# A fused attention and feed-forward kernel: v split one operand per step and passed on through DRAM, seven products in the second layer from a pair's first step on

## The chip, the cores and the metric

The kernel runs on one core of a Trainium2 chip. The metric is the device time of one execution in microseconds (us). The engines are named as in the profile: PE multiplies matrices (PEld loads its weights), DVE and ACT work on vectors, POOL is not used here, and SP issues the transfers (DMA) through one queue.

## The reference

Four batches of 6080 tokens with 256 channels pass through a channel attention and then through a feed-forward network with 2048 hidden units.

```python
# attention: q, k, v are (4, 6080, 256), scores are 256 x 256 per batch
qn = q / (norm(q, axis=1) + 1e-06)
kn = k / (norm(k, axis=1) + 1e-06)
a = softmax(kn.T @ qn / tau)
x = v @ a
# feed-forward, w_in 256 x 2048, w_out 2048 x 256
h = x @ w_in
out = 0.5 * h * (1 + erf(h / sqrt(2))) @ w_out
```

All is float32.

## The kernel before

**Numbers.** Each float32 operand of a product is split into a high part (a cast on ACT) and a low part (a difference on DVE), and a product is three passes on PE: high by high, high by low, low by high. The attention is folded into the first layer: for each batch, softmax(scores) times w_in gives that batch's first weights, so that the first layer is v times these.

**Tiles.** A pair is two blocks of n = 512 tokens (480 in a batch's last pair); each batch has six, written (b,p). A pair runs through eight steps u; in a step two tiles of 128 hidden units are made. So there are 192 steps, (b,p,u). Within a step PE's code alternates between the first layer of step u and the second layer of the step before: `slot` 0 to 6 count the seven products of the first layer (`first_products`, `do(0)` to `do(6)`, by the table `ORDER`), and after each of them one or two groups of `second_products` are put in, each of three matmuls. Behind every step come the stages `EDGE` and `EDGE + 1`.

**Seven products.** The first layer is one level of Strassen's scheme in Winograd's form: seven products of half blocks in place of eight, 21 matmuls of n columns. It needs seven operands from v: the blocks B11, B21, B22 and the sums T1 to T4 (`v_sum`), each split (`v_split`) into tiles vh and vl. In pair (0,0) `plain_products` makes the first layer with eight products from B11, B21, B12, B22. The second layer has four groups for the token block j = 1 (12 matmuls of n columns), then for j = 0 either four more plain groups (12 matmuls of n columns) or the same scheme with seven products (21 matmuls of n/2 columns, on `ws`, sums of w_out, and on sums of the hidden values that `sums` makes on DVE and ACT). `strassen(b,p,u)` says which: seven products for all u but 0, from pair (0,2) on.

**Accumulators.** The plain groups add into the PSUM tiles c10, c11 (j = 1) and c00, c01 (j = 0), the seven products into p0, p1 and also into c00 and c01. Behind a pair's last step `evict` copies c10 and c11 out (in step u=0 of the next pair), and in its step u=1 `combine` forms the results of p0 and p1 in osb (one copy on ACT, four operations on DVE) and `merge` adds c00 and c01 to it. Only then may the next pair write these tiles.

**v.** `load_v` brings 1 MB of a pair's v into v_raw; the four sums are made in steps u=3 to 6 of the pair before, and the seven splits in its step u=7 and the next pair's step u=0, each shortly after the product that last used the old tile.

**Other work beside it.** While a batch runs, the scores of the next are gathered: `load_qk`, `split_qk` (tiles hl) and `burst` (16 matmuls between two steps), `norm_part` (norms of the columns), `softmax`, and the next batch's first weights (`w_part`, `w_split`). In batch 3 there is none of this. The weights w_out of a step (wo, 512 KB, and ws, 512 KB) are read back from DRAM for every step by `ahead`, wo two steps and ws one step before use; there are two buffers of each.

**Order.** `at(step, slot, job)` puts a job behind a slot, `run` calls it there, and `spread` puts the stages of a generator behind later slots (12 is slot 2 of the next step). From pair (0,1) on the orders of PE, DVE and ACT are those in which the code issues; the order of SP's queue is found by a scheduler from a model of its own.

Of the kernel before, what the change touches and what calls it, by code (L numbers as in the profile page):

```python
# [9 lines left out]
F32 = mybir.dt.float32  # L10
F32R = mybir.dt.float32r
# [3 lines left out]
ALU = mybir.AluOpType  # L15
AX = mybir.AxisListType

P = 128
B, N, C = 4, 6080, 256
DFF = 2048  # L20
NT = 512
NJ = -(-N // P)
NFT = DFF // P
NCT = C // P
# [41 lines left out]
def channel_attention_gelu_ffn(ctx, tc, qk, kqt, vt, tau, w_in, w_out, out):  # L66
# [29 lines left out]
    def f32(ap):  # L96
        return ap.bitcast(F32)
# [405 lines left out]

    def load_v(b, p):
        t0, n = PAIRS[p]
        raw = pv.tile([P, NCT, 2 * NT], F32, name="v_raw")
        nc.sync.dma_start(out=raw[:, :, :2 * n],
                          in_=vt[:, b * N + t0:b * N + t0 + 2 * n].rearrange("(t p) n -> p t n", p=P))
        vraw[b, p] = raw

    def v_blocks(b, p):
        n = PAIRS[p][1]
        raw = vraw[b, p]
        return {(k, j): raw[:, k, j * n:(j + 1) * n] for k in range(2) for j in range(2)}

    def v_sum(b, p, i):
        n = PAIRS[p][1]
        x = v_blocks(b, p)
        if i == 0:
            vts[b, p] = [pv.tile([P, NT], F32, name=f"vs{k}") for k in range(4)]  # L520
        ts = [t[:, :n] for t in vts[b, p]]
        to, x0, x1 = ((0, x[0, 1], x[0, 0]), (2, x[1, 1], x[0, 1]), (1, x[1, 1], ts[0]), (3, x[1, 0], ts[1]))[i]
        dve.tensor_tensor(out=ts[to], in0=x0, in1=x1, op=ALU.subtract)

    def v_split(b, p, i):
        n = PAIRS[p][1]
        x = v_blocks(b, p)
        src = {B11: x[0, 0], B21: x[1, 0], B22: x[1, 1]}.get(i)
        if (b, p) == (0, 0) and i == B12:
            src = x[0, 1]  # L530
        if src is None:
            src = vts[b, p][i - T1][:, :n]
        hi = pv.tile([P, NT], F32R, name=f"vh{i}")
        lo = pv.tile([P, NT], F32R, name=f"vl{i}")
        vops[b, p, i] = hi, lo
        act.copy(out=hi[:, :n], in_=src)
        yield
        dve.tensor_tensor(out=lo[:, :n], in0=src, in1=f32(hi[:, :n]), op=ALU.subtract)

# [11 lines left out]
        passes(ps[:, :n], whs[g][:, a, q], wls[g][:, a, q], hi[:, :n], lo[:, :n], start, stop)  # L553

    def strassen(b, p, u):
        return u > 0 and (b, p) > (0, 1) and (b, p, u) != (B - 1, NP - 1, NU - 1)

    pending = []

# [103 lines left out]
    def plain_products(b, p, u):  # L663

        n = PAIRS[p][1]
        g, q = divmod(u, 2)
        out = state["blocks"] = {}
        wh, wl = whs[g], wls[g]
        a21 = a21s[g]
        rows = {1: ((wh[:, A11, q], wl[:, A11, q]), (wh[:, A12, q], wl[:, A12, q])),  # L670
                0: ((a21[:, 0, q], a21[:, 1, q]), (wh[:, A22, q], wl[:, A22, q]))}
        cols = {0: (B11, B21), 1: (B12, B22)}
        for j in (1, 0):
            for i in (1, 0):
                ps = bank()
                for k in range(2):
                    hi, lo = vops[b, p, cols[j][k]]
                    passes(ps[:, :n], *rows[i][k], hi[:, :n], lo[:, :n], k == 0, k == 1)
                    if k == 0:
                        yield  # L680
                out[i, j] = gelu(ps[:, :n], n, i, j)
                flush()
                if (i, j) != (0, 0):
                    yield
# [93 lines left out]
    def merge(b, p, c):  # L778

        n = PAIRS[p][1]  # L780
        po = pos[b, p]
        last = (b, p) == (B - 1, NP - 1)
        parts = ((0, n // 2), (n // 2, n)) if last and c == NCT - 1 else ((0, n),)
        for lo, hi in parts:
            y = po["y"][:, c, lo:hi]
            dve.tensor_tensor(out=y, in0=po[f"c0{c}"][:, lo:hi], in1=y, op=ALU.add)
            if last:
                t = b * N + PAIRS[p][0]
                nc.sync.dma_start(out=out[c * P:(c + 1) * P, t + lo:t + hi], in_=y)
        if c == NCT - 1 and not last:  # L790
            store(b, p, 0, po["y"])
# [62 lines left out]
    for js in range(NQS):  # L854
# [5 lines left out]
            load_unit()  # L860
        if js in NARROWS:
            narrow_unit()
    for i in (B11, B21, B12, B22):
        deque(v_split(0, 0, i), 0)
    for x in held:
        keep(*x)
    fill = qk_fill()
# [53 lines left out]
    def at(step, slot, job):  # L921
        jobs.setdefault((step, slot), []).append(job)
# [5 lines left out]
    def spread(gen, step, *slots):  # L928
        for x in slots:
            at(step + x // 10, x % 10, lambda: next(gen, None))  # L930
# [20 lines left out]
        at(s + 1, EDGE, drop)  # L951
    for b in range(1, B):
        base = (b - 1) * NP * NU
        for i in range(2 * NCT * NSC):

            def norm(b=b, i=i, step=base + 8 + i):
                gen = norm_part(b, *divmod(i, NSC))
                with behind("kept"):
                    next(gen)
                at(step + 1, 2, lambda: next(gen, None))  # L960
            at(base + 8 + i, EDGE, norm)

        def soft(step=base + 36):
            gen = softmax(False)
            next(gen)
            spread(gen, step, 12, 10 + EDGE, 22, 26, 20 + EDGE)
        at(base + 36, EDGE, soft)
        for g in range(NWG):
            at(base + 39 + 2 * g, EDGE if g == 0 else EDGE + 1, lambda b=b, g=g: load_win(b, g))
            for m in range(NCT):  # L970
                at(base + 41 + 2 * g + m, EDGE, lambda b=b, g=g, m=m: w_part(b, g, m))

            def wsums(b=b, g=g, step=base + 42 + 2 * g):
                spread(w_split(b, g), step, 10, 11, 12, 20, 22, 23)
            at(base + 42 + 2 * g, EDGE, wsums)
    for b in range(B):
        for p in range(NP):
            nxt = (b, p + 1) if p + 1 < NP else (b + 1, 0)
            base = (b * NP + p) * NU
            if nxt[0] < B:  # L980
                at(base + 1, EDGE, lambda nxt=nxt: load_v(*nxt))
                for i in range(4):
                    at(base + 3 + i, 6, lambda nxt=nxt, i=i: v_sum(*nxt, i))
                for i, (hi, lo) in enumerate(((1, 2), (2, 3), (3, 4), (5, 6), (6, 10), (10, 11), (11, 12))):

                    def vs(nxt=nxt, i=i, step=base + NU - 1, lo=lo):
                        gen = v_split(*nxt, ORDER[i][1])
                        next(gen)
                        spread(gen, step, lo)
                    at(base + NU - 1 + hi // 10, hi % 10, vs)  # L990
                if (b, p) > (0, 1):

                    def end(b=b, p=p, step=base + NU + 1):
                        gen = combine(b, p)
                        next(gen)
                        spread(gen, step, 1)
                        for c in range(NCT):
                            at(step, 2, lambda c=c: merge(b, p, c))
                    at(base + NU + 1, 0, end)

    steps = [(b, p, u) for b in range(B) for p in range(NP) for u in range(NU)]
    second, count, rest = iter(()), 0, iter(())
# [70 lines left out]
```

## Time and profile before

| | us |
|---|---|
| runs shown | 2173.92, 2174.5, 2175.94 (median 2174.5) |
| the profiled execution | 2174.69 |
| its span | 2172.9 |
| PE busy | 2152.8 |
| DVE busy | 1734.9 |
| ACT busy | 1622.5 |

The time of an execution lies 1.8 us over its profile's span. Busy shares are means over very different stages: the first 61 us are loads, norms and the first batch's scores; pair (0,0) follows until 154 us, pair (0,1) until 244 us, and the other 22 pairs run in the same pattern until the end. A plain step takes about 10.4 us, or 11.8 with a burst of scores behind it. A row of the timeline has start, duration, engine, line, operation, the tiles written and read, and their shapes; what stands in brackets is the idle time before it and what ended it. Since one helper records every operation, all rows of the engines have the line L138, and one goes by the tiles; rows of SP have the lines of their own.

### The profile page before, as it was taken

Reading aid. Unit: us, or ns where it says so; the run is one execution under the profiler, and the core shown is the slowest. Engines: PE = TensorE matmul, PEld = TensorE weight load, DVE = VectorE, ACT = ScalarE, POOL = GpSimd, SP = SyncE. Lnnn points to the kernel's source line nnn. Section 1 sums busy time; section 2 is a strip of 40 time slices with the busy share of each in tenths; the row PEclk is TensorE's granted clock in tenths of the full one; section 3 lists DMA queues with packets and bytes.
Section 4 is the critical chain, followed back from the end, with each engine's and each line's share of the span. In section 5 each row is a group of like instructions: output and inputs, shape, how many; then the busy total and the mean of one; then the engine's idle time right before and its main releaser. Section 6 shows DMA issues by size and latency. Waiting matters only on the chain.

```text
span 2172.9 us, 29906 instructions
## 1 busy us (share of the span) xinstructions
PE 2152.8 (99%) x11061; PEld 1822.7 (84%) x11061; DVE 1734.9 (80%) x2732; ACT 1622.5 (75%) x2692; POOL 1.3 (0%) x8
## 2 busy tenths in 40 slices
PE   9999999999999999999999999999999999999999
PEld 8777888887888888888888888888888888888888
DVE  6997788877788788887788878888778777777776
ACT  5767778867777787786777778887677777677675
POOL 0000000000000000000000000000000000000000
PEclk9999999999999999999999999999999999999999
DMA  9545655544344555553434545554344333333332
GB/s 381 180 150 199 213 184 199 183 161 146 136 144 145 176 204 180 199 202 128 140 135 141 173 168 202 184 205 163 106 146 144 118 129 114 127 128 115 125 119 95
DMA packets 100547, 352.18 MB, mean 162 GB/s; under 512 B 10288, under 2 KB 12464, under 8 KB 98352
## 3 DMA queue, kind: packets, MB, share of 16 engines
q1 hardware_dynamic: 100400, 350.27, 46.3%
q8 instruction: 87, 1.43, 0.3%
q14 instruction: 60, 0.49, 0.1%
HBM read 312.74 MB, written 37.49 MB: 161 GB/s over the span
## 4 chain that ended last, share of the span: by engine, by line
PE 87%; DVE 7%; ACT 4%; issue 1%; DMA 0%; DVEq 0%; ACTq 0%; POOL 0%; POOLq 0%
PE h L138 45%; PE c L138 33%; PE p L138 9%; DVE h L138 2%; DVE vl L138 2%; DVE x L138 1%; ACT gh L138 1%; DVE gl L138 1%; ACT x L138 1%; ACT vh L138 1%; ACT g L138 0%; DVE small L138 0%; ACT L138 0%; ACT p L138 0%; DVE osb L138 0%
## 5 line engine op out<-in xcount | busy, mean ns | idle before, releaser
L138 PE MATMUL c<-gh,wo 128*128 128x512 f32 (+3 forms) x2460 | 870.4, 364 | 0.4 <-DVE wo L138 0.4
L138 PE MATMUL h<-vh,wh 128*128 128x512 f32 (+1 forms) x1312 | 520.3, 397 | 12.9 <-DVE h L138 2.8
L138 PEld LDWEIGHTS c<-gh,wo 128*128 128x128 f32 x2460 | 462.2, 188 | 81.9 <-DVE wo L138 1.5
L138 PE MATMUL h<-vh,wl 128*128 128x512 f32 (+1 forms) x1312 | 513.5, 391 | 0.0
L138 PE MATMUL h<-vl,wh 128*128 128x512 f32 (+1 forms) x1312 | 513.5, 391 | 0.0
L138 ACT ACTIVATE gh<-h 128x512 fp32r<-128x512 f32 (+1 forms) x446 | 277.9, 623 | 238.2 <-DVE h L138 219.2
L138 PE MATMUL c<-gl,wo 128*128 128x512 f32 (+3 forms) x1230 | 443.8, 361 | 0.1
L138 DVE TENSOR_TENSOR gl<-x,gh 128x768 fp32r<-128x768 f32 (+3 forms) x306 | 329.8, 1078 | 63.5 <-ACT gh L138 63.3
L138 DVE TENSOR_TENSOR gl<-g,gh 128x512 fp32r<-128x512 f32 (+1 forms) x462 | 314.5, 681 | 49.3 <-ACT g L138 47.1
L138 DVE TENSOR_TENSOR h<-h,p 128x512 f32<-128x512 f32 (+1 forms) x368 | 251.4, 683 | 79.5 <-PE h L138 68.3
L138 ACT COPY p<-h 128x512 f32<-128x512 f32 (+1 forms) x368 | 213.7, 581 | 126.3 <-PE h L138 126.2
L138 PEld LDWEIGHTS h<-vh,wh 128*128 128x128 f32 x1312 | 247.0, 188 | 72.3 <-ACT p L138 9.2
L138 ACT CAST gh<-x 128x768 fp32r<-128x768 f32 (+3 forms) x306 | 286.8, 937 | 16.7 <-DVE x L138 11.7
L138 PEld LDWEIGHTS h<-vh,wl 128*128 128x128 f32 x1312 | 246.4, 188 | 51.9
L138 DVE TENSOR_TENSOR x<-x 128x256 f32<-128x256 f32 (+4 forms) x491 | 241.1, 494 | 52.5 <-ACT x L138 34.8
L138 PEld LDWEIGHTS h<-vl,wh 128*128 128x128 f32 x1312 | 246.7, 188 | 35.4
L138 ACT ACTIVATE g<-h 128x512 f32<-128x512 f32 (+1 forms) x446 | 271.6, 609 | 0.0
L138 PEld LDWEIGHTS c<-gl,wo 128*128 128x128 f32 x1230 | 231.0, 188 | 45.3 <-DVE gl L138 0.5
L138 ACT ACTIVATE x<-h 128x512 f32<-128x512 f32 (+1 forms) x306 | 182.3, 609 | 48.9 <-DVE h L138 47.8
L138 PE MATMUL p<-gh,ws 128*128 128x256 f32 (+1 forms) x918 | 210.2, 280 | 0.0
L138 DVE TENSOR_TENSOR h<-h,u 128x512 f32<-128x512 f32 (+1 forms) x184 | 125.8, 684 | 83.5 <-PE h L138 82.6
L138 PEld LDWEIGHTS p<-gh,ws 128*128 128x128 f32 x918 | 162.6, 189 | 6.8
(153 smaller groups left out, 2229.5 us busy)
## 6 DMA issues: line engine op xcount, KB each, us to landing
wo<-keep_out SPq DMA_DIRECT2D x184, 512.0 KB, 4.5
ws<-keep_sum SPq DMA_DIRECT2D x153, 512.0 KB, 3.7
raw<-qk SPq DMA_DIRECT2D x94, 512.0 KB, 4.5
raw<-kqt SPq DMA_DIRECT2D x72, 512.0 KB, 4.6
v_raw<-vt SPq DMA_DIRECT2D x20, 1024.0 KB, 5.0
out<-osb SPq DMA_DIRECT2D x40, 512.0 KB, 3.9
hl<-keep_in SPq DMA_DIRECT2D x12, 1024.0 KB, 5.4
raw<-w_in SPq DMA_DIRECT2D x8, 512.0 KB, 6.9
```

The source lines that it names most:

```text
L138: r = op(*args, **kw)
```

## The change

- `strassen` no longer leaves out u = 0: from pair (0,2) on 22 more steps have seven products in the second layer.
- One operand of v is split per step: for the next pair's operand `ORDER[i]` in step u = i, the cast on ACT into a tile vp behind slot 5, the difference on DVE in place (in v_raw or vs) behind slot 3 of the next step (slot 6 for i = 0). Both halves are stored to DRAM (keep_v, two sets of seven) and fetched into vh and vl by 14 transfers of 256 KB that are issued in step u = 7 behind the product that last used the old tile. The sums of v have two buffers in place of four and stand in steps 0, 2, 3 and 4, and v_raw is loaded in step 7 of the pair before that.
- `end`: combine behind slots 1 and 2 of step u=1 in place of 0 and 1; the merges of c00 and c01 behind slots 2 and 3 in place of both behind 2; that of c01 adds half the columns.
- The 24 pieces of `norm_part` per batch go to the steps with the fewest splits of scores, within a wider range of steps.
- In pair (0,0) `plain_products` takes the blocks j in the order 0, 1, and B12's split tiles are those of T4.

On DVE, in step u=1 of pair (0,3): gl are low halves of hidden values, hl the split scores, h sums of the first layer, p and c the accumulators. Before:

```order
L138 TENSOR_TENSOR gl_3335<-g,gh_3334 128x512
L138 TENSOR_TENSOR sacc<-h_3367,sacc 128x512
L138 TENSOR_TENSOR gl_3350<-g,gh_3349 128x512
L138 TENSOR_TENSOR osb<-p_2604,osb 128x256
L138 TENSOR_TENSOR osb<-p_2619,osb 128x256
L138 TENSOR_TENSOR osb<-osb,p_2619 128x256 x2
L138 TENSOR_TENSOR osb<-c_2503,osb 128x512
L138 TENSOR_TENSOR osb<-c_2515,osb 128x512
L138 TENSOR_TENSOR hl<-raw,hl 128x1024
L138 TENSOR_TENSOR h<-h_3396,u_3413 128x512
```

And now:

```order
L138 TENSOR_TENSOR sacc<-h_3503,sacc 128x512
L138 TENSOR_TENSOR x<-x 128x256
L138 TENSOR_TENSOR gl_3493<-x,gh_3492 128x768
L138 TENSOR_TENSOR gl_3495<-x,gh_3494 128x1024
L138 TENSOR_TENSOR osb<-p_2601,osb 128x256
L138 TENSOR_TENSOR osb<-p_2616,osb 128x256
L138 TENSOR_TENSOR hl<-raw,hl 128x1024
L138 TENSOR_TENSOR osb<-osb,p_2616 128x256 x2
L138 TENSOR_TENSOR osb<-c_2597,osb 128x512
L138 TENSOR_TENSOR h<-h_3530,u_3550 128x512
L138 TENSOR_TENSOR osb<-c_2632,osb 128x256
```

The sums of x and their two low halves now stand ahead of the combine, and hl stands ahead of the merge in place of behind it; the second merge is half as wide and stands behind h.

On ACT, at the same place (p and u are copies of the first layer's sums, raw the loaded scores). Before:

```order
L138 COPY p_3385<-h_3381 128x512
L138 COPY osb<-p_2604 128x256
L138 COPY p_3400<-h_3396 128x512
L138 CAST hl<-raw 128x1024
L138 COPY u_3413<-h_3381 128x512
```

And now:

```order
L138 COPY p_3522<-h_3518 128x512
L138 CAST gh_3494<-x 128x1024
L138 COPY p_3534<-h_3530 128x512
L138 CAST hl<-raw 128x1024
L138 COPY osb<-p_2601 128x256
L138 COPY u_3550<-h_3518 128x512
```

A cast of the sums has come in, and the combine's copy moved behind the cast of hl.

In SP's queue, at the end of a pair of batch 3. The names keep_out_96 and keep_sum_104 to 111 are the stored w_out and ws, keep_v_0 to keep_v_6 the operands B11, B21, B22, T1, T2, T3, T4. Before there are wo and ws in turn, and between them v_raw and the outputs:

```order
L310 DMA ws<-keep_sum_111 128x1024
L300 DMA wo<-keep_out_103 128x1024
L310 DMA ws<-keep_sum_105 128x1024
L300 DMA wo<-keep_out_96 128x1024
L507 DMA v_raw<-vt 128x2x1024
L761 DMA out<-osb 128x2x512
```

And now:

```order
L556 DMA vh_19714<-keep_v_2_114 128x512
L300 DMA wo<-keep_out_96 128x1024
L557 DMA vl_19715<-keep_v_2_114 128x512
L548 DMA keep_v_6_118<-vp 128x512
L549 DMA keep_v_6_118<-vs 128x512
L556 DMA vh_19738<-keep_v_5_117 128x512
L557 DMA vl_19739<-keep_v_5_117 128x512
L556 DMA vh_19756<-keep_v_1_113 128x512
L557 DMA vl_19757<-keep_v_1_113 128x512
L556 DMA vh_19773<-keep_v_6_118 128x512
L557 DMA vl_19774<-keep_v_6_118 128x512
```

The first wo of the next pair stands between the two halves of B22, ahead of T3, B21 and T4; the last stores of the pair stand there too.

```diff
@@ -503,8 +503,8 @@
 
     def load_v(b, p):
         t0, n = PAIRS[p]
-        raw = pv.tile([P, NCT, 2 * NT], F32, name="v_raw")
-        nc.sync.dma_start(out=raw[:, :, :2 * n],
+        raw = pv.tile([P, NCT, 2 * NT], F32R, name="v_raw")
+        nc.sync.dma_start(out=f32(raw[:, :, :2 * n]),
                           in_=vt[:, b * N + t0:b * N + t0 + 2 * n].rearrange("(t p) n -> p t n", p=P))
         vraw[b, p] = raw
 
@@ -516,26 +516,45 @@
     def v_sum(b, p, i):
         n = PAIRS[p][1]
         x = v_blocks(b, p)
-        if i == 0:
-            vts[b, p] = [pv.tile([P, NT], F32, name=f"vs{k}") for k in range(4)]
-        ts = [t[:, :n] for t in vts[b, p]]
-        to, x0, x1 = ((0, x[0, 1], x[0, 0]), (2, x[1, 1], x[0, 1]), (1, x[1, 1], ts[0]), (3, x[1, 0], ts[1]))[i]
-        dve.tensor_tensor(out=ts[to], in0=x0, in1=x1, op=ALU.subtract)
+        ts = vts.setdefault((b, p), {})
+        to, x0, x1 = ((T1, x[0, 1], x[0, 0]), (T2, x[1, 1], ts.get(T1, x)), (T4, x[1, 0], ts.get(T2, x)),
+                      (T3, x[1, 1], x[0, 1]))[i]
+        x0, x1 = f32(x0), f32(x1 if i in (0, 3) else x1[:, :n])
+        ts[to] = pv.tile([P, NT], F32R, name="vs", bufs=2)
+        dve.tensor_tensor(out=f32(ts[to][:, :n]), in0=x0, in1=x1, op=ALU.subtract)
+
+    keep_v = [[pdram.tile([P, 2, NT], F32, name=f"keep_v{k}_{i}") for i in range(7)] for k in range(2)]
+
+    def v_first(i, name):
+        n = PAIRS[0][1]
+        src = v_blocks(0, 0)[{B11: (0, 0), B21: (1, 0), B22: (1, 1), B12: (0, 1)}[i]]
+        hi = pv.tile([P, NT], F32R, name=f"vh{name}")
+        lo = pv.tile([P, NT], F32R, name=f"vl{name}")
+        vops[0, 0, i] = hi, lo
+        act.copy(out=hi[:, :n], in_=f32(src))
+        dve.tensor_tensor(out=lo[:, :n], in0=f32(src), in1=f32(hi[:, :n]), op=ALU.subtract)
 
     def v_split(b, p, i):
         n = PAIRS[p][1]
         x = v_blocks(b, p)
         src = {B11: x[0, 0], B21: x[1, 0], B22: x[1, 1]}.get(i)
-        if (b, p) == (0, 0) and i == B12:
-            src = x[0, 1]
         if src is None:
-            src = vts[b, p][i - T1][:, :n]
+            src = vts[b, p][i][:, :n]
+        hi = pv.tile([P, NT], F32R, name="vp", bufs=2)
+        act.copy(out=hi[:, :n], in_=f32(src))
+        yield
+        dve.tensor_tensor(out=src, in0=f32(src), in1=f32(hi[:, :n]), op=ALU.subtract)
+        to = keep_v[p % 2][i]
+        nc.sync.dma_start(out=to[:, 0, :n], in_=f32(hi[:, :n]))
+        nc.sync.dma_start(out=to[:, 1, :n], in_=f32(src))
+
+    def v_fetch(b, p, i):
+        n = PAIRS[p][1]
         hi = pv.tile([P, NT], F32R, name=f"vh{i}")
         lo = pv.tile([P, NT], F32R, name=f"vl{i}")
         vops[b, p, i] = hi, lo
-        act.copy(out=hi[:, :n], in_=src)
-        yield
-        dve.tensor_tensor(out=lo[:, :n], in0=src, in1=f32(hi[:, :n]), op=ALU.subtract)
+        nc.sync.dma_start(out=f32(hi[:, :n]), in_=keep_v[p % 2][i][:, 0, :n])
+        nc.sync.dma_start(out=f32(lo[:, :n]), in_=keep_v[p % 2][i][:, 1, :n])
 
 
 
@@ -553,7 +572,7 @@
         passes(ps[:, :n], whs[g][:, a, q], wls[g][:, a, q], hi[:, :n], lo[:, :n], start, stop)
 
     def strassen(b, p, u):
-        return u > 0 and (b, p) > (0, 1) and (b, p, u) != (B - 1, NP - 1, NU - 1)
+        return (b, p) > (0, 1) and (b, p, u) != (B - 1, NP - 1, NU - 1)
 
     pending = []
 
@@ -670,7 +689,7 @@
         rows = {1: ((wh[:, A11, q], wl[:, A11, q]), (wh[:, A12, q], wl[:, A12, q])),
                 0: ((a21[:, 0, q], a21[:, 1, q]), (wh[:, A22, q], wl[:, A22, q]))}
         cols = {0: (B11, B21), 1: (B12, B22)}
-        for j in (1, 0):
+        for j in (0, 1):
             for i in (1, 0):
                 ps = bank()
                 for k in range(2):
@@ -781,6 +800,8 @@
         po = pos[b, p]
         last = (b, p) == (B - 1, NP - 1)
         parts = ((0, n // 2), (n // 2, n)) if last and c == NCT - 1 else ((0, n),)
+        if c == NCT - 1 and all(strassen(b, p, u) for u in range(NU)):
+            parts = ((n // 2, n),)
         for lo, hi in parts:
             y = po["y"][:, c, lo:hi]
             dve.tensor_tensor(out=y, in0=po[f"c0{c}"][:, lo:hi], in1=y, op=ALU.add)
@@ -860,8 +881,8 @@
             load_unit()
         if js in NARROWS:
             narrow_unit()
-    for i in (B11, B21, B12, B22):
-        deque(v_split(0, 0, i), 0)
+    for i, name in ((B11, B11), (B21, B21), (B12, T4), (B22, B22)):
+        v_first(i, name)
     for x in held:
         keep(*x)
     fill = qk_fill()
@@ -951,14 +972,20 @@
         at(s + 1, EDGE, drop)
     for b in range(1, B):
         base = (b - 1) * NP * NU
-        for i in range(2 * NCT * NSC):
-
-            def norm(b=b, i=i, step=base + 8 + i):
+        split_at = {}
+        for k in range(FIRSTB if b == 1 else 0, NQS // NB):
+            for t in range(NB):
+                x = bursts.get((b, k - 1), bursts[b, k] - 3) + 1 + t
+                split_at[x] = split_at.get(x, 0) + 1
+        free = sorted(range(base + (9 if b == 1 else 2), base + 35), key=lambda x: (x % NU == 0, split_at.get(x, 0), x))
+        for i, x in enumerate(sorted(free[:2 * NCT * NSC])):
+
+            def norm(b=b, i=i, step=x):
                 gen = norm_part(b, *divmod(i, NSC))
                 with behind("kept"):
                     next(gen)
-                at(step + 1, 2, lambda: next(gen, None))
-            at(base + 8 + i, EDGE, norm)
+                at(step, 2, lambda: next(gen, None))
+            at(x - 1, EDGE, norm)
 
         def soft(step=base + 36):
             gen = softmax(False)
@@ -978,25 +1005,33 @@
             nxt = (b, p + 1) if p + 1 < NP else (b + 1, 0)
             base = (b * NP + p) * NU
             if nxt[0] < B:
-                at(base + 1, EDGE, lambda nxt=nxt: load_v(*nxt))
-                for i in range(4):
-                    at(base + 3 + i, 6, lambda nxt=nxt, i=i: v_sum(*nxt, i))
-                for i, (hi, lo) in enumerate(((1, 2), (2, 3), (3, 4), (5, 6), (6, 10), (10, 11), (11, 12))):
-
-                    def vs(nxt=nxt, i=i, step=base + NU - 1, lo=lo):
-                        gen = v_split(*nxt, ORDER[i][1])
+                for i, (step, slot) in enumerate(((0, 6), (2, 0), (3, 0), (4, 0))):
+                    at(base + step, slot, lambda nxt=nxt, i=i: v_sum(*nxt, i))
+                for i, (_, x) in enumerate(ORDER):
+
+                    def vs(nxt=nxt, x=x, i=i, step=base + i):
+                        gen = v_split(*nxt, x)
                         next(gen)
-                        spread(gen, step, lo)
-                    at(base + NU - 1 + hi // 10, hi % 10, vs)
+                        spread(gen, step, 16 if i == 0 else 13)
+                    at(base + i, 5, vs)
+                fetch = [(i, i) for i in range(7)]
+                if (b, p) == (0, 0):
+                    load_v(*nxt)
+                    fetch = [(0, 1), (0, 2), (4, 0), (4, 5), (6, 4), (6, 3), (6, 6)]
+                for slot, i in fetch:
+                    at(base + NU - 1, slot, lambda nxt=nxt, i=i: v_fetch(*nxt, ORDER[i][1]))
+                after = (nxt[0], nxt[1] + 1) if nxt[1] + 1 < NP else (nxt[0] + 1, 0)
+                if after[0] < B:
+                    at(base + NU - 1, EDGE, lambda after=after: load_v(*after))
                 if (b, p) > (0, 1):
 
                     def end(b=b, p=p, step=base + NU + 1):
                         gen = combine(b, p)
                         next(gen)
-                        spread(gen, step, 1)
+                        spread(gen, step, 2)
                         for c in range(NCT):
-                            at(step, 2, lambda c=c: merge(b, p, c))
-                    at(base + NU + 1, 0, end)
+                            at(step, 2 + c, lambda c=c: merge(b, p, c))
+                    at(base + NU + 1, 1, end)
 
     steps = [(b, p, u) for b in range(B) for p in range(NP) for u in range(NU)]
     second, count, rest = iter(()), 0, iter(())
```

## The prediction

> **What bounds the kernel now.** I read the page first (its busy shares and its chain), then the span by steps, then the rows of single steps on DVE, ACT and SP.
>
> ```profile
> span 2172.9 us, 29906 instructions
> PE 2152.8 (99%) x11061; PEld 1822.7 (84%) x11061; DVE 1734.9 (80%) x2732; ACT 1622.5 (75%) x2692; POOL 1.3 (0%) x8
> ...
> q1 hardware_dynamic: 100400, 350.27, 46.3%
> ...
> PE 87%; DVE 7%; ACT 4%; issue 1%; DMA 0%; DVEq 0%; ACTq 0%; POOL 0%; POOLq 0%
> ```
>
> PE is busy for 99% and carries 87% of the chain. So an edit pays only if it shortens PE's own row of matmuls, or takes away one of the short waits in it, and it costs wherever it makes PE wait. The profiled execution took 2174.69 us, the median of the runs is 2174.5: I add the sum to the median.
>
> The next windows are single steps of the two layers; the columns are start:end, length, then busy time and count of PE, PEld, DVE, ACT and POOL, the granted clock (1.00 all through), the DMA share and GB/s.
>
> ```profile
> 345.32:357.18 11.86, 11.86 (x55) 9.78 (x55) 9.53 (x16) 8.07 (x14) 0.00 (x0) 1.00 0.81 276
> 357.18:368.68 11.50, 11.50 (x65) 9.88 (x63) 8.74 (x12) 8.87 (x14) 0.00 (x0) 1.00 0.44 139
> 527.48:538.70 11.22, 11.22 (x53) 9.49 (x52) 9.02 (x17) 7.05 (x13) 0.00 (x0) 1.00 0.53 175
> 538.70:549.62 10.92, 10.92 (x61) 9.68 (x60) 6.30 (x11) 7.27 (x12) 0.00 (x0) 1.00 0.39 151
> 1852.21:1862.64 10.43, 10.43 (x47) 8.37 (x46) 8.11 (x14) 7.11 (x13) 0.00 (x0) 1.00 0.52 177
> 1862.64:1872.73 10.09, 10.09 (x56) 8.66 (x55) 6.59 (x11) 6.65 (x12) 0.00 (x0) 1.00 0.14 52
> ```
>
> They are steps u=1 and u=2 of pairs (0,3), (0,5) and (3,2). Step u=1 holds the plain second layer of u=0, step u=2 the seven-product one of u=1, with the same first layer. The seven products are 0.36, 0.30 and 0.34 us shorter.
>
> **What the change gains.** First, 22 pairs run the second layer of u=0 with seven products too: 18 at about 0.35 and four of the shorter pairs at 0.30, 7.5 us, and the few hundredths of waits in those steps bring it to 7.9. Second, the steps u=0:
>
> ```profile
> 243.80:255.67 11.87, 11.87 (x53) 9.72 (x54) 9.65 (x15) 10.25 (x19) 0.00 (x0) 1.00 0.82 286
> ...
> 604.14:616.86 12.72, 12.12 (x62) 9.46 (x61) 11.70 (x19) 10.94 (x20) 0.00 (x0) 1.00 0.60 208
> ...
> 1841.69:1852.20 10.51, 10.37 (x56) 8.58 (x55) 9.65 (x15) 9.31 (x17) 0.00 (x0) 1.00 0.67 226
> ...
> 2086.19:2096.37 10.18, 10.08 (x56) 8.59 (x55) 9.41 (x16) 8.92 (x17) 0.00 (x0) 1.00 0.42 157
> sum 248.89, PE 244.82 PEld 200.81 DVE 226.86 ACT 222.24 POOL 0.00; mean PE 11.13 PEld 9.13 DVE 10.31 ACT 10.10 POOL 0.00
> ```
>
> These are the first and last of the 22, two between, and the sum. The same matmuls at the pace of the undisturbed steps (10.09 without scores, 11.48 with, and the odd ones by their counts) take 235.8, so 13.1 us of these steps is waiting. DVE and ACT are at 10.3 and 10.1 of 11.3 there: seven splits of v fall on u=7 and u=0. One split per step takes most of them out; I leave 0.6 for the steps (b,0,0), whose other work stays. Gain 12.5. The start of (0,2,0) waits 0.9 before it for the same splits: gone too. Gains together 21.3.
>
> The price of spreading: 28 transfers of 256 KB in each of 23 pairs, 169 MB on 350, so q1's 46.3% becomes about 69%. Through most of a pair that is hidden, because the loads of weights have half a step to spare. SP's 672 new issues at the 0.41 us between two issues (rows below) are 276 us of a queue that mostly waits for buffers.
>
> **Cost one: the merge stands behind the new chain.** With seven products in u=0, step u=1 begins with their operand sums on DVE, and PE's first product of the second half, c00, is the one that needs the old c0 merged away. It comes after 27 matmuls of 512 columns at 0.231 us, S+6.24 (S is the step's start). How long the chain takes is read from step (0,3,2), S=357.18, which has such sums now, and the combine from (0,3,1):
>
> ```profile
> 347.21 0.89 DVE L138 TENSOR_TENSOR osb<-p,osb 128x256 f32<-128x256 f32 x2 [0.48 <-ACT osb L138]
> 348.13 0.75 DVE L138 TENSOR_TENSOR osb<-osb,p 128x256 f32<-128x256 f32 x2
> 348.92 1.29 DVE L138 TENSOR_TENSOR osb<-c,osb 128x512 f32<-128x512 f32 x2
> 350.12 1.22 DVE L138 TENSOR_TENSOR hl<-raw,hl 128x1024 fp32r<-128x1024 f32 x1
> 351.25 0.69 DVE L138 TENSOR_TENSOR h<-h,u 128x512 f32<-128x512 f32 x1
> ...
> 358.32 0.95 DVE L138 TENSOR_TENSOR gl<-x,gh 128x768 fp32r<-128x768 f32 x1
> 359.63 1.23 DVE L138 TENSOR_TENSOR gl<-x,gh 128x1024 fp32r<-128x1024 f32 x1 [0.36 <-ACT gh L138]
> ```
>
> ```profile
> 358.55 1.05 ACT L138 CAST gh<-x 128x1024 fp32r<-128x1024 f32 x1
> 359.50 0.59 ACT L138 COPY p<-h 128x512 f32<-128x512 f32 x1
> 359.97 1.06 ACT L138 CAST hl<-raw 128x1024 fp32r<-128x1024 f32 x1
> 360.93 0.60 ACT L138 COPY u<-h 128x512 f32<-128x512 f32 x1
> ```
>
> In the new order ACT's copy for the combine stands behind the cast of hl: it starts at 360.93, S+3.75, and 0.38 later DVE may begin. DVE is free from gl at about S+3.6. So: two combine operations from S+4.17 (0.92 to the next start), the hl difference from about S+5.0 (1.13), two more combine operations (0.79), and the merge of c0 from S+6.9, 0.69 long: S+7.6. PE asks at 6.24 and waits 1.4 us. So it goes in seven steps with an hl split ((0,3), (1,2..4), (2,2..4)), and, with four sums of scores in the same place, in (1,0), (2,0), (3,0): 10 × 1.4 = 14. In the other 11 no hl stands between; there DVE's gl starts at S+2.5 as in this row of b=3 (S=1872.73),
>
> ```profile
> 1875.23 1.23 DVE L138 TENSOR_TENSOR gl<-x,gh 128x1024 fp32r<-128x1024 f32 x1 [0.25 <-ACT gh L138]
> ```
>
> and about 0.4 later with the new v cast and v difference ahead. Combine 1.7 and merge 0.69 after its end at S+4.0 give S+6.4 to 6.6: a wait of 0.35. 11 × 0.35 = 3.9. Sum 17.9. Bounds: no wait in the 11 and 0.9 in the ten, 9; 0.9 and 2.0, 30. I take 17.9, as each piece has a row. Queued behind the merge on DVE is h<-h,u, which frees the bank of PE's sixth product: it ends 0.6 after the merge, before PE, itself late, comes to it.
>
> **Cost two: the fetch stands behind wo.** In SP's order the load of wo for the buffer that u=6's second layer reads, which is free only when step 7 ends, stands ahead of the fetches of T3, B21 and T4 and, in five pairs, of B22.
>
> ```profile
> 1709.57 0.32 SPq L310 DMA_DIRECT2D ws<-keep_sum  x1
> 1709.98 0.38 SPq L300 DMA_DIRECT2D wo<-keep_out  x1
> 1719.66 0.32 SPq L310 DMA_DIRECT2D ws<-keep_sum  x1
> ```
>
> ```profile
> wo<-keep_out SPq DMA_DIRECT2D x184, 512.0 KB, 4.5
> ws<-keep_sum SPq DMA_DIRECT2D x153, 512.0 KB, 3.7
> ...
> out<-osb SPq DMA_DIRECT2D x3, 240.0 KB, 2.0
> ```
>
> ```profile
> 10.00:20.00 10.00, 10.00 (x48) 8.81 (x47) 8.58 (x7) 8.27 (x10) 0.00 (x0) 1.00 1.03 414
> ```
>
> wo, issued 0.41 after ws, lands 1.2 after it: 0.6 per 256 KB; at the 414 GB/s of 10 to 20 us it is 0.63. I take 0.65, and 2.4 for the rest of a transfer (3.7 less 1.3). From the step's end E, wo (two units of 256 KB), B22's second half, two stores and T3's two halves are seven units: 4.55 + 2.4 = E+7.0. PE comes to T3 after 25 matmuls, E+5.77. In the four fetches inside b=3 that is 1.2 each, 4.9. Where steps are longer or the stores come later I get 0.45 in five pairs and 0.5 in one: 2.7. Together 7.6, with 0 as the lower end (the queue works at several transfers at once) and 18 as the upper (a microsecond more in all ten).
>
> By the Trainium skill, "DMA: Bandwidth & Descriptors", section Specifications, a core has some 358 GB/s of HBM; the row of 414 does not agree, so I stay with the row. With 358 this term would grow by an estimated 0.5 us in each of ten pairs, 5 us.
>
> **Costs three and four.**
>
> ```profile
> 106.00:119.00 13.00, 13.00 (x58) 10.58 (x57) 12.68 (x26) 8.41 (x17) 0.00 (x0) 1.00 0.38 122
> 119.00:132.00 13.00, 12.57 (x54) 9.52 (x53) 12.99 (x26) 8.28 (x18) 0.00 (x0) 1.00 0.43 162
> 627.33:637.71 10.38, 10.37 (x56) 8.67 (x55) 9.74 (x13) 8.02 (x13) 0.00 (x0) 1.00 0.32 102
> ```
>
> In pair (0,0) DVE has no slack (12.7 and 13.0 of 13), and about six more operations of 0.6 now fall into it rather than into its end: 3.6 of DVE, of which I put 2 on PE (0 to 4). The order j=0 first costs nothing by itself. In (1,0,2) and (2,0,2) DVE is at 9.7 of 10.4 and gets two more: 2 us (0 to 3). The moved pieces of the norm are the same operations in steps with fewer splits: nothing, as a step like (0,3,2) leaves DVE 2.8 us and ACT 2.6; where that cover is gone a piece costs PE at most its one operation, about 1 us. Costs together 17.9 + 7.6 + 2 + 2 = 29.5.
>
> **Sum.** −21.3 + 29.5 = +8.2: 2174.5 + 8.2 = 2182.7, about 2183.
>
> **The rivals.**
> - The merge is in time. If ACT makes its copy ahead of the hl cast or DVE's four combine operations slip into gaps of the sums, c00 doesn't wait: −21.3 + 11.6 = −9.7, 2165. It decides where the wait, over 21 steps, falls below a mean of 0.46 us. For it: DVE is idle for 2.3 us of (0,3,1) even now (9.53 of 11.86). Against it: both queues are in the order shown, and each piece ahead has a duration above.
> - The fetches come in time and half the wait for the merge is real: −21.3 + 9 + 4 + 4 = −4.3, just at the edge of what a measurement tells from nothing, 0.2% or 4.3 us; with the fetches as costed it is −0.7. About 2172.
> - Transfers of 256 KB are slower than I take them. At half of 414 GB/s a unit is 1.3 and T3 lands at E+11.5: 5.7 us late in place of 1.2 in the four pairs of b=3 alone, +18, and 2183 becomes 2201 or more. Against it: the 240 KB row lands after 2.0. By the Trainium skill, the same page, section Bandwidth, 64 KB reaches 138 GB/s and 1 MB 341, and it asks for transfers of 1 MiB; its figures were for another issuing engine, and by an estimate between them 256 KB has about 240.
>
> **How the numbers follow.** The waits as costed: 0.45 (2178 to 2190 by itself). The merge in time: 0.2. The half case: 0.25. Slow transfers: 0.1. Faster by over 0.2% takes the second: 0.2; within 0.2% the third: 0.25; slower the first and last: 0.55. The range goes from 2163, just past the merge in time, to 2193, where the waits for the merge are near their upper bound; beyond lie most of the last case and the tails.
>
> **What would show it.** In the profile after, steps u=0 should be clean (10.1 or 11.5), and PE's matmul p or c of steps u=1 should show an idle stretch of about 1.4 in ten pairs, ended by DVE's osb<-c. In b=3, PE's h<-vh of the fifth product in u=0 should start 1.2 late behind a landing vl. If neither wait is there, the faster rival holds; if vl's landing is far beyond E+7, the last one does.

## The result and the profile after

The changed kernel takes 2252.3 us (median; 2246.2 to 2253.9 in four runs) against 2175.1 of the kernel before: a ratio of 1.035, 95% interval 1.033 to 1.037. It is 77 us slower; 8 slower were forecast, with 2193 as the upper end.

The page after:

```profile
span 2250.4 us, 31601 instructions
...
PE 2169.2 (96%) x11259; PEld 1826.1 (81%) x11259; DVE 1777.8 (79%) x2798; ACT 1636.1 (73%) x2692; POOL 1.3 (0%) x8
...
q1 hardware_dynamic: 196304, 528.83, 68.7%
...
PE 74%; DMA 10%; DVE 7%; ACT 6%; issue 2%; SPq 1%; DVEq 0%; ACTq 0%
```

DMA was 0% of the chain that ended last and is 10% now. PE, 99% busy before, is at 96%.

The steps u=0 and, below their sum, two steps u=1, as windows with the columns of the prediction:

```profile
353.87:368.12 14.25, 12.69 (x64) 9.73 (x63) 9.96 (x14) 8.82 (x14) 0.00 (x0) 1.00 0.90 311
...
631.65:643.98 12.33, 12.12 (x61) 9.37 (x60) 9.42 (x14) 9.38 (x15) 0.00 (x0) 1.00 1.01 358
...
1909.79:1924.06 14.27, 11.14 (x57) 8.48 (x55) 8.13 (x13) 8.10 (x14) 0.00 (x0) 1.00 0.88 290
...
sum 285.96, PE 254.17 PEld 201.89 DVE 195.05 ACT 185.46 POOL 0.00; mean PE 11.55 PEld 9.18 DVE 8.87 ACT 8.43 POOL 0.00
```

```profile
368.12:381.11 12.99, 11.75 (x64) 9.81 (x63) 11.02 (x18) 9.27 (x16) 0.00 (x0) 1.00 0.90 305
...
1924.06:1934.18 10.12, 10.12 (x57) 8.59 (x56) 9.41 (x17) 6.60 (x12) 0.00 (x0) 1.00 0.54 184
```

DVE fell to 8.9 us in a step u=0 (10.3 before), as meant, and yet the 22 steps take 286.0 us in place of 248.9. What ends PE's waits there is named by the groups of waits (from 257 us on; us in total, times, longest):

```profile
PEld h L138 <- DMA vl<-keep_v: 30.7, 50, 1.8
...
PEld c L138 <- DVE osb L138: 15.4, 10, 1.7
...
PE h L138 <- DMA vl<-keep_v: 13.6, 15, 1.5
...
PE c L138 <- DVE osb L138: 12.3, 14, 1.3
...
PE h L138 <- DMA vh<-keep_v: 10.4, 17, 0.8
```

PEld and PE rows can cover the same moment, so these are not added. There are two kinds: the fetched halves of v, and the merge (DVE osb). The next table separates them by steps. A step's wait is its length less its matmuls at the pace of undisturbed steps, as in the prediction (0.231 us for 512 columns, 0.118 for 256, 0.217 and 0.112 for 480 and 240); each column sums it over all pairs for the profiled execution of that kernel. What PE loses by a lower clock (last section) is in it too. Executions of one kernel with stores and fetches lie 5 to 11 us apart (after, e3, e4, e5, e9), so a difference of a few us between such columns is not firm.

| waits, us | before | after | e1 no fetch | e3 wo late | e9 first piece | e5 merges early | e6 v at home | e7 both | e10 hl late |
|---|---|---|---|---|---|---|---|---|---|
| pair (0,0) | 2.1 | 7.1 | 7.0 | 7.0 | 7.1 | 7.1 | 2.2 | 2.2 | 2.1 |
| pair (0,1) | 2.0 | 10.5 | 13.2 | 11.4 | 9.1 | 11.2 | 3.0 | 2.3 | 2.2 |
| u=0 | 13.1 | 50.2 | −0.1 | 10.3 | 36.3 | 48.5 | 11.6 | 11.6 | 11.6 |
| u=1 | 1.6 | 23.6 | 20.7 | 28.3 | 25.8 | 12.4 | 19.1 | 9.8 | 5.1 |
| u=2 | 0.5 | 6.4 | 5.0 | 8.0 | 7.2 | 7.6 | 2.0 | 2.3 | 4.3 |
| u=3 to 7 | 13.2 | 18.7 | 18.2 | 18.5 | 19.7 | 20.0 | 13.2 | 13.3 | 13.3 |
| matmuls | 2107.9 | 2101.6 | 2101.6 | 2101.6 | 2101.6 | 2101.6 | 2101.6 | 2101.6 | 2101.6 |

After against before: u=0 +37, u=1 +22, the first two pairs +13.5, u=2 +6, the rest +5.5, matmuls −6.3: 78, against 77.5 between the two spans.

**The waits of u=0.** The next rows are the boundary between (3,1) and (3,2), where u=0 starts at 1909.79. SP's queue:

```profile
1905.38 0.32 SPq L556 DMA_DIRECT2D vh<-keep_v  x1
1909.98 0.32 SPq L300 DMA_DIRECT2D wo<-keep_out  x1
1910.35 0.42 SPq L557 DMA_DIRECT2D vl<-keep_v  x1
1910.87 0.38 SPq L548 DMA_DIRECT2D keep_v<-vp  x1
1911.34 0.38 SPq L549 DMA_DIRECT2D keep_v<-vs  x1
...
1914.18 0.53 SPq L557 DMA_DIRECT2D vl<-keep_v  x1
1916.03 0.32 SPq L556 DMA_DIRECT2D vh<-keep_v  x1
1916.69 0.32 SPq L557 DMA_DIRECT2D vl<-keep_v  x1
```

PE in the same step:

```profile
1915.37 0.51 PE L138 MATMUL h<-vl,wh 128*128 128x512 f32 x1 [1.04 <-DMA vl<-keep_v]
...
1917.41 0.47 PE L138 MATMUL h<-vh,wh 128*128 128x512 f32 x1 [0.61 <-DMA vh<-keep_v]
...
1922.42 0.50 PE L138 MATMUL h<-vl,wh 128*128 128x512 f32 x1 [1.39 <-DMA vl<-keep_v]
```

SP stands still for 4.3 us before wo, which waits for a buffer until step 7 ends; half of B22 and all of T3, B21 and T4 are issued behind it. PE then waits three times, for B22, T3 and T4. T4's fetch, the last, also has to wait for T4's two stores: issued at 1910.87 and 1911.34, they land 5.1 and 5.3 us later, and the two halves of T4 are issued right after that, at 1916.03 and 1916.69.

### The profile page after: what moved, and what is told of

The parts are those of the page before. It is cut to its first block, busy times and chain, and to the rows that moved or that the text cites. A ratio compares the mean times of both kernels' runs of the same rounds, so it can differ in the third digit from the quotient of the medians.

```text
span 2250.4 us, 31601 instructions
## 1 busy us (share of the span) xinstructions
PE 2169.2 (96%) x11259; PEld 1826.1 (81%) x11259; DVE 1777.8 (79%) x2798; ACT 1636.1 (73%) x2692; POOL 1.3 (0%) x8
## 4 chain that ended last, share of the span: by engine, by line
PE 74%; DMA 10%; DVE 7%; ACT 6%; issue 2%; SPq 1%; DVEq 0%; ACTq 0%
PE h L138 39%; PE c L138 25%; PE p L138 10%; DMA vl<-keep_v 4%; DMA keep_v<-vs 2%; ACT gh L138 2%; DVE osb L138 2%; DVE x L138 1%; DVE h L138 1%; ACT x L138 1%; DMA wo<-keep_out 1%; DMA vh<-keep_v 1%; DMA raw<-kqt 1%; DVE hl L138 1%; ACT g L138 1%
## 5 line engine op out<-in xcount | busy, mean ns | idle before, releaser
L138 PE MATMUL c<-gh,wo 128*128 128x512 f32 (+3 forms) x2372 | 828.9, 360 | 15.0 <-DVE osb L138 12.3
L138 ACT ACTIVATE gh<-h 128x512 fp32r<-128x512 f32 (+1 forms) x402 | 251.3, 625 | 290.0 <-DVE h L138 280.0
L138 DVE TENSOR_TENSOR x<-x 128x256 f32<-128x256 f32 (+2 forms) x557 | 275.0, 496 | 178.3 <-ACT x L138 168.3
L138 DVE TENSOR_TENSOR gl<-x,gh 128x768 fp32r<-128x768 f32 (+1 forms) x350 | 376.9, 1077 | 47.3 <-ACT gh L138 47.2
L138 ACT CAST gh<-x 128x768 fp32r<-128x768 f32 (+1 forms) x350 | 327.8, 937 | 34.6 <-DVE x L138 28.8
L138 DVE TENSOR_TENSOR gl<-g,gh 128x512 fp32r<-128x512 f32 (+1 forms) x418 | 283.7, 680 | 39.0 <-ACT g L138 35.8
L138 ACT ACTIVATE x<-h 128x512 f32<-128x512 f32 (+1 forms) x350 | 212.0, 607 | 59.3 <-DVE h L138 53.4
L138 ACT ACTIVATE g<-h 128x512 f32<-128x512 f32 (+1 forms) x402 | 245.1, 610 | 0.0
L138 PE MATMUL p<-gh,ws 128*128 128x256 f32 (+1 forms) x1050 | 240.3, 280 | 0.0
L138 PEld LDWEIGHTS p<-gh,ws 128*128 128x128 f32 x1050 | 185.9, 189 | 7.7
```

Source lines behind the costliest of these rows:

```text
L138: r = op(*args, **kw)
```

## The experiments

The first four take the change apart where PE waits.

**e1: no fetches.**

```diff
     def v_fetch(b, p, i):
+        if (b, p) > (0, 1):
+            vops[b, p, i] = fetched[i]
+            return
```

> Fetches of v left out from pair (0,2) on: the vh and vl of pair (0,1) are used for all later pairs (so the values are not the reference's); splits and stores stay. If the fetches cause the waits of the steps u=0 (50.2 us over the pace of their matmuls in the changed kernel, 13.1 before), these fall to about 5 us and the time to 2252 - 45 = 2207 or a little lower (the late norm loads of (0,2,0) come in time as well); the 22 us of the steps u=1 stay. If DVE's and ACT's new work of u=0 causes them, less than half goes: 2230 or more.

2198.3 us, 54 less than the changed kernel. The 22 steps u=0 sum to the pace of their matmuls:

```profile
sum 235.71, PE 235.71 PEld 203.42 DVE 190.25 ACT 180.93 POOL 0.00; mean PE 10.71 PEld 9.25 DVE 8.65 ACT 8.22 POOL 0.00
```

So all 50 us of waits in u=0 hang on the fetches, and without them the 13 us of before are gone as well: the split of one operand per step does on DVE and ACT what it was costed to do.

**e2: no stores.**

```diff
         dve.tensor_tensor(out=src, in0=f32(src), in1=f32(hi[:, :n]), op=ALU.subtract)
+        if (b, p) > (0, 2):
+            return
         to = keep_v[p % 2][i]
```

> Stores of v left out after the first pairs: later fetches bring the first pairs' operands again (so the values are not the reference's), splits and fetches stay. If the queue is full around step 7 and u=0, the two stores of T4 that stand among the fetches (1.3 us at 0.65 each) and the fetch of T4 that has to wait for them are worth 1 to 2 us in some 16 pairs: 2252 - 16 to 32 = 2220 to 2236. If the fetches alone are too late by their own order and latency, under 6 us.

2204.9 us, 47 less and so a larger gain than either reading gave; u=0 has 3.9 us of waits, all of them in (0,2), whose operands are still stored. This run doesn't tell the two apart: with the stores gone, SP's order changed too, and wo came to stand behind T3 and B22, ahead of B21 and T4 alone. SP still stands still before wo (2.8 us at the boundary between (3,1) and (3,2)), but PE doesn't wait there. So the halt alone is not enough: it costs by what stands behind it.

**e3: wo behind the fetches.** The load of wo for u=0 moves from the end of step 6 to the end of step 7.

```diff
-        nxt = after(2)
-        if nxt[0] < B and nxt[:2] != (0, 0):
-            load_wo(nxt)
+        for k in ((), (1, 2), (2,))[1 if u == NU - 1 else 0 if u == NU - 2 else 2]:
+            nxt = after(k)
+            if nxt[0] < B and nxt[:2] != (0, 0):
+                load_wo(nxt)
```

> The load of wo for u=0 is asked for at the end of step 7 and so stands behind all fetches of v in SP's order. If it is wo's place alone that makes the fetches late (as the prediction had it), the waits of u=0 go to some 8 us: 2252 - 40 = 2212. If the queue is full whatever the order, the fetches behind it gain its 1.3 us once in some 16 pairs, about 20 us: 2232, and the wait of the first operands stays.

2219.3 us, 33 less, and u=0's waits are 10.3 us. In SP's queue the same boundary (u=0 at 1887.53) now has no such halt:

```profile
1884.74 0.32 SPq L557 DMA_DIRECT2D vl<-keep_v  x1
...
1891.41 0.32 SPq L557 DMA_DIRECT2D vl<-keep_v  x1
1891.78 0.42 SPq L300 DMA_DIRECT2D wo<-keep_out  x1
```

40 of the 50 us go with wo's place. u=1 has 5 more (28.3 in place of 23.6), where wo is now late itself: in (2,0,1) PE waits 1.94 us for it. 9 of the other 10 lie in batches 0 to 2, where score loads share the queue.

**e9: only the first 32 KB of wo in the old place.** The other 480 KB go behind the fetches.

```diff
+            if u == NU - 2:
+                new_wo(nxt)
+                piece(nxt, 0, 0, slice(0, 64))
...
+        if nxt[0] < B and u == NU - 1:
+            piece(nxt, 0, 0, slice(64, C))
+            piece(nxt, 0, 1)
+            piece(nxt, 1)
```

> The changed kernel with wo of u=0 loaded in pieces: the first 32 KB where the whole load stood in SP's queue, with its wait for the buffer, the other 480 KB behind all fetches. If the 512 KB ahead of the fetches are what makes them late, this goes the way of the late load, to 2220. If it is SP that stands still until step 7 ends, with all fetches behind it, the waits of u=0 stay at 35 to 50 us and the time at 2235 to 2252.

2237.7 us, and u=0's waits are 36.3. The halt in SP's queue is as it was (u=0 at 1902.97):

```profile
1899.04 0.32 SPq L556 DMA_DIRECT2D vh<-keep_v  x1
1903.17 0.32 SPq L928 DMA_DIRECT2D wo<-keep_out  x1
1903.54 0.43 SPq L557 DMA_DIRECT2D vl<-keep_v  x1
```

So of the 40 us that wo's place costs, about 26 (36.3 less 10.3) are the halt with all fetches behind it and 14 the half megabyte ahead of them. The split is rough: four of e9's steps u=0 ran in part at half clock (granted 0.89 to 0.95 over the step), which by estimate is some 5 us of the 36; one of the changed kernel's did (0.89) and none of e3's. Without that the parts are about 20 and 18.

**e4: u=0's second layer plain again**, with combine and merges at their old slots.

```diff
-        return (b, p) > (0, 1) and (b, p, u) != (B - 1, NP - 1, NU - 1)
+        return u > 0 and (b, p) > (0, 1) and (b, p, u) != (B - 1, NP - 1, NU - 1)
```

> The plain second layer for u=0 again, combine and merges at their old slots; v, norm pieces and pair (0,0) as in the changed kernel. If the parts add, the 22 us of the steps u=1 go and 6.2 us of matmuls come back: 2252 - 16 = 2236, and u=0 keeps its waits of about 50. If the sums for u=0's second layer have a share in the waits of u=0 as well, it is faster than 2230.

2225.3 us (2219.8 to 2230.8, a wide spread). u=1's waits are 3.8 us, so the 20 us there come with the seven products in u=0 and with the later combine and merges (this run takes back both); u=0 keeps 42.9. The median is below 2230, as the second reading had it, but with executions 11 us apart it stays open whether the sums have a share in the waits of u=0.

**e5: combine and merges early.**

```diff
-                        spread(gen, step, 2)
+                        spread(gen, step, 0)
                         for c in range(NCT):
-                            at(step, 2 + c, lambda c=c: merge(b, p, c))
-                    at(base + NU + 1, 1, end)
+                            at(step, c, lambda c=c: merge(b, p, c))
+                    at(base + NU, EDGE, end)
```

> The changed kernel with the combine behind step u=0 (EDGE) and behind slot 0 of u=1, the merges behind slots 0 and 1, that is ahead of the low halves of u=0's sums on DVE and ahead of the cast of hl on ACT. If PE's wait in the steps u=1 (23.6 us over the pace, 1.6 before) is DVE's and ACT's order, c00 no longer waits; h<-h,u, which frees the bank of the sixth product, now ends last, at S+7.3 by the rows (PE asks at S+6.94), so some 0.4 stays in ten steps: 2252 - 18 = 2234. If DVE is simply too full there, the wait moves to that bank whole and less than 6 us go.

2243.1 us: 9 less, half of what was expected. u=1 gains 11.2 (23.6 to 12.4), but u=2 to u=7 have 2.5 more, 1.3 of it in the one step (0,2,7). c00 doesn't wait any more in (0,3,1); PE waits for the bank that h<-h,u frees:

```profile
376.20 0.51 PE L138 MATMUL h<-vh,wh 128*128 128x512 f32 x1 [0.44 <-DVE h L138]
```

```profile
374.33 1.21 DVE L138 TENSOR_TENSOR hl<-raw,hl 128x1024 fp32r<-128x1024 f32 x1
375.47 0.68 DVE L138 TENSOR_TENSOR h<-h,u 128x512 f32<-128x512 f32 x1
```

**e6: v as before, the rest of the change kept.** Splits, sums and pair (0,0) are the old code; `strassen`, `end`, `merge` and the norm pieces are the new one.

> v as in the kernel before (splits in u=7 and u=0, no store, no fetch), pair (0,0) as before; u=0's second layer with seven products, combine and merges as in the changed kernel, norm pieces too. If the parts add: 2175 - 6 (matmuls) + 21 (waits for the merge in u=1) and the 13 us of waits in u=0 stay: 2190. If the bunched splits and the new sums for u=0's second layer meet on DVE in u=0 (10.3 of 11.3 us busy before), 2 us more in each of 22 pairs: 2230.

2185.4 us (ratio to before 1.0047, 1.0032 to 1.0062). The first two pairs are as before to within 1 us, u=0 has 11.6 and u=1 19.1 us of waits. The second layer's part of the change thus costs 10 us where v is as before, and v's part (one split per step, the passage through DRAM, pair (0,0)) another 67 (2252.3 less 2185.4): together the 77. The two parts don't simply add. By e4, v's part alone costs 50 (2225.3 less 2175.1) and the second layer's 27 on top of it.

**e7: e6 with the combine and merges early; e10: and hl's low half behind slot 4 in the steps u=1.**

```diff
-                at(step, 2, lambda: next(gen, None))
+                at(step, 4 if step % NU == 1 else 2, lambda: next(gen, None))
             at(prev + 1 + t, 1, split)
```

> As the one before (v as in the kernel before), with the combine and the merges early as well. If the wait for the merge is only order, 18 us less than that run: 2172, a little faster than before. If DVE is too full, no faster than 2184.

> As e7 (v as in the kernel before, seven products for u=0, merges early, norm pieces moved), and in the steps u=1 the low half of hl on DVE stands behind slot 4 in place of slot 2, that is behind h<-h,u. If hl is what keeps PE's sixth product waiting in seven of those steps (0.6 each in e7's trace), 4 to 5 us less than e7: 2172, faster than before by some 0.1%. If another operation then ends last, no change to e7, 2177.

e7 takes 2177.0 us (1.0009, 0.9999 to 1.0018), between its two readings, and e10 2174.7 (0.9997, 0.9988 to 1.0006). u=1's waits fall from 19.1 to 9.8 to 5.1; u=2 takes 2.0 of the last 4.7 back; why was not taken apart. Against the kernel before, e10's profile has 6.3 us less of matmuls and 1.5 less of waits in u=0, but 7.5 more in (0,1), u=1 and u=2: the gain is given back.

**e8: the changed kernel with wo late and the merges early.**

> The changed kernel with wo of u=0 behind the fetches and the merges early. The two waits are independent by their places, so the gains add: 2252 - 33 - 18 = 2201. If they share cover (a late step u=0 gives DVE time), 5 to 10 us less is gained.

2212.2 us; 7 less than e3, not 18. u=1 still has 17.0 us of waits: as in e5, the bank behind h<-h,u takes the merge's place (0.7 in six steps), and in four steps of pairs with score loads 1.2 to 2.4 remain.

**e11: the norm pieces alone; e12: e10 with the old norm places.**

> The kernel before with the norm pieces in the steps of the changed kernel, nothing else. By the steps u=0 of e6 and e7 (11.6 us of waits against 13.1) about 1 us faster, 2174, within what can be told from nothing; if the pieces in steps u=2 and 3 of a batch's first pair meet the sums of scores there, up to 3 us slower.

> As e10 with the norm pieces where they were in the kernel before. If the moved pieces are worth 1 us, 2173; if they cost the waits in step u=2 of a batch's first pair (0.8 us each in e7), 2171.

2174.95 us (0.999 to 1.0008) and 2174.98 (0.9991 to 1.0008): the moved pieces change nothing that can be told. No version that was run beats the kernel before.

## Why the prediction was wrong, step by step

- **The direction** was right, and not by luck: e1, with no fetch to wait for, is still 23 us slower than the kernel before. The largest cost was taken at a sixth of itself.
- **Gains.** Matmuls: 7.9 forecast, 6.3 by the counts; the step lengths from which it was taken hold 0.02 to 0.08 of waits each. The old waits of u=0: 12.5 forecast, 13.2 shown by e1. The wait ahead of (0,2,0) did not go; it grew (0.9 to 3.8). (SP's 672 new issues should be 644, 28 in each of 23 pairs; nothing in the sum hangs on it.)
- **Cost one, the merge**: 17.9 forecast, 20.7 in e1, where nothing else disturbs u=1 and the ten steps that were named lose 1.5 to 1.6 each. The chain came as it was built from rows; (0,3,1), where S is 368.12:

```profile
370.58 1.23 DVE L138 TENSOR_TENSOR gl<-x,gh 128x1024 fp32r<-128x1024 f32 x1 [0.36 <-ACT gh L138]
372.28 0.88 DVE L138 TENSOR_TENSOR osb<-p,osb 128x256 f32<-128x256 f32 x2 [0.48 <-ACT osb L138]
373.08 1.21 DVE L138 TENSOR_TENSOR hl<-raw,hl 128x1024 fp32r<-128x1024 f32 x1
374.22 0.74 DVE L138 TENSOR_TENSOR osb<-osb,p 128x256 f32<-128x256 f32 x2
374.99 0.69 DVE L138 TENSOR_TENSOR osb<-c,osb 128x512 f32<-128x512 f32 x1
```

```profile
375.74 0.39 PE L138 MATMUL c<-gh,wo 128*128 128x256 f32 x1 [1.24 <-DVE osb L138]
```

  The combine starts at S+4.16 (4.17 forecast), the merge ends at S+7.56 (7.6), and PE's gap is 1.41. The claim that h<-h,u is no later than PE held only while PE waited for the merge; e5 shows it next in line.
- **Cost two, the fetch behind wo, is the step that failed**: 7.6 forecast with 18 as its upper end, 50 measured. The place was right (e3). So was the pace of a full queue: in (3,2,0) T3 and B21 are issued in a row and land some 0.65 apart, so the third rival's slow transfers are not the cause. Three things were mis-sized.
  - The sum priced one operand per pair, T3, at 1.2 us. In (3,2,0) PE waits for B22, T3 and T4, and the step loses 4.2. T4 stood in no term: its second half, issued at 1916.69 behind its stores, lands 5.7 us later, 12.6 us behind the step's start E.
  - The sum let SP begin at E and took 2.4 us and 0.65 for each 256 KB ahead. By that B22's second half lands at E+4.35; issued at 1910.35 and landing 5.0 us later, it came at E+5.6. T3 was whole at E+8.1, not E+7.0. With wo's half megabyte away the same sum gives E+5.7 for T3, before PE asks for it, and so no cost; e9 still has 36 us of waits in u=0, 20 to 26 more than e3.
  - In batches 0 to 2 it allowed some 0.5 in each of at most six pairs. There the steps u=0 wait 1.5 to 3.5 in eleven of the 16 pairs, 5.6 in (0,2) and nothing in the three short ones.
- **Costs three and four.** Pair (0,0): 2 forecast (0 to 4), 5.0. Steps (1,0,2) and (2,0,2): 2 forecast, 3.3, and (3,0,2), not forecast, 1.0. Pair (0,1) was not priced at all and costs 8.5; e6 takes back v and pair (0,0)'s own edits and brings both pairs back to within 1 us, so they come with these.
- **What stood in no term.** Loads of other kinds are late too, and DVE and ACT, whose order is fixed, stand with them. ACT waits for a norm load five times, 16.6 us in all (never before, nor in e1 from 257 us on); the longest is in (0,2,0), where the load stands behind wo and six fetches:

```profile
268.52 1.06 ACT L138 ACTIVATE raw<-raw 128x1024 f32<-128x1024 f32 x1 [6.11 <-DMA raw<-kqt]
```

  In (0,1,7) DVE waits for a wo:

```profile
248.93 0.69 DVE L138 TENSOR_TENSOR x<-wo 128x512 f32<-128x512 f32 x1 [4.99 <-DMA wo<-keep_out]
```

  This one isn't due to the fetches. They stand behind that wo; what is ahead of it is the 1 MB of v_raw, which the change loads in steps u=7 (u=1 before):

```profile
240.74 0.38 SPq L507 DMA_DIRECT2D v_raw<-vt  x1
241.22 0.42 SPq L300 DMA_DIRECT2D wo<-keep_out  x1
242.79 0.33 SPq L556 DMA_DIRECT2D vh<-keep_v  x1
```

  And in e1, where the fetches of that step are gone, DVE waits as long (whether v_raw's place causes it was not tested):

```profile
248.20 0.69 DVE L138 TENSOR_TENSOR x<-wo 128x512 f32<-128x512 f32 x1 [5.22 <-DMA wo<-keep_out]
```

  The prediction said that a norm piece costs PE at most its own operation. That is true of the operation, not of its load.
- **Left open.** Some 10 us of waits in u=0 that stay with wo late (e3) were not taken apart; nor was which of v's operations makes (0,0) and the steps u=5 and 6 (+4.3) longer.

## What to carry to other kernels

When a change puts a chain of transfers into a queue that works in order, look for the one entry that waits for a buffer: everything behind it starts only when that buffer is free, and each consumer behind it may wait, not only the first. A fetch of what the same queue has just stored is a chain of its own, since it can't be issued before the store has landed. Price a fetch for all its consumers, and against the queue's load in that stretch (here 280 to 360 GB/s in u=0) instead of its mean over the span (q1 at 69%). And a stall that an operation shift removes is worth what is second in the line: taking c00's wait away gave half of it, because the bank's release came next.

## What the runs showed of the hardware

The queue did not always move bytes at one pace. The windows stand in the boundary above: just behind the halt, in the full stream, and some 2 us after T4's fetch had waited for its stores.

```profile
1911.00:1913.60 2.60, 2.60 (x13) 2.13 (x12) 2.27 (x3) 1.89 (x4) 0.00 (x0) 1.00 0.85 250
1914.50:1918.00 3.50, 1.93 (x7) 1.08 (x7) 1.31 (x2) 1.28 (x3) 0.00 (x0) 1.00 1.05 387
1918.60:1920.60 2.00, 2.00 (x16) 1.85 (x15) 1.76 (x3) 1.14 (x2) 0.00 (x0) 1.00 0.96 205
```

387 GB/s in the stream, 250 and 205 in the other two, with the engines' busy share at 0.85 and 0.96. Both lie behind a gap in SP's issues, but that a queue run dry is the cause isn't shown. In e2 the engines were busy throughout (share 1.05 from 1869 to 1871 us, 1.06 and 1.17 in the next two), and yet the last of these microseconds moved only 283 GB/s. Nor did the halt empty the queue at once: in the changed kernel it still moved 383 GB/s from 1909 to 1910 us, at the halt's end, and 170 in the microsecond after.

A long wait also costs PE its clock. In (0,2,0) PE waited for 4 us, and what came next ran at a granted clock of 0.50:

```profile
272.08 2.92 PE L138 MATMUL h<-hl 128*128 128x512 f32 x8 [4.09 <-DVE h L138]
```

```profile
272.00:274.00 2.00, 1.92 (x6) 1.63 (x7) 2.00 (x5) 1.94 (x4) 0.00 (x0) 0.50 1.05 343
...
277.00:278.00 1.00, 1.00 (x4) 0.81 (x3) 0.11 (x1) 0.86 (x1) 0.00 (x0) 0.51 0.98 301
278.00:279.00 1.00, 1.00 (x5) 0.83 (x5) 1.00 (x1) 0.45 (x1) 0.00 (x0) 1.00 0.97 344
```

From 272.1 to 278.0, 5.9 us at half speed, it lost some 3 us on top of the 4. The length of the wait alone doesn't decide: in (2,1,1) 1.95 us had the same effect, while 3.50 us in (0,1,7) left the clock at 1.00.

```profile
1301.93 2.92 PE L138 MATMUL h<-hl 128*128 128x512 f32 x8 [1.95 <-DVE h L138]
```

```profile
1302.00:1303.00 1.00, 1.00 (x3) 0.90 (x4) 1.00 (x2) 1.00 (x2) 0.00 (x0) 0.50 0.68 262
```

```profile
252.46 0.50 PE L138 MATMUL h<-vh,wh 128*128 128x512 f32 x1 [3.50 <-DVE h L138]
```

```profile
254.00:256.00 2.00, 2.00 (x10) 1.64 (x9) 1.52 (x3) 1.78 (x4) 0.00 (x0) 1.00 0.38 143
```

By the Trainium skill, "TensorE: Matmul & The Clock Gate", section Part 1, the clock is halved after at least one idle window of about 3.4 us, on a window that runs freely. The row of (0,2,0) agrees with that, the row of (2,1,1) does not.
